# Two chained attention blocks on one core: one weight quarter loaded earlier, six weight pieces later, and the second output projection started eight units later

## The chip, the cores and the metric

The kernel runs on one core of a Trainium2 chip. The metric is the device time of one execution in microseconds (us); lower is better. A kernel with rounds is compared with the kernel before on the same chip in the same rounds. One execution of each kernel was taken by the hardware profiler.

Engines in the profile: PE is the matrix engine (PEld its weight loads), ACT the scalar engine, DVE the vector engine, POOL the general engine, SP the engine that issues all loads and stores. SPq is SP's queue.

## The reference, cut to what matters

Two independent problems A and B of the same shape; their outputs are put side by side.

```python
B, Sq, D = 16, 144, 448          # batch, queries, model width
H, Sk, Dh = 16, 512, 256         # heads, cached keys, head width
q = (x @ wq).reshape(B, Sq, H, Dh).transpose(0, 2, 1, 3)
scores = jnp.einsum("bhqd,bhkd->bhqk", q, k_cache) * (Dh ** -0.5)
p = softmax(scores)
o = jnp.einsum("bhqk,bhkd->bhqd", p, v_cache)
y = o.transpose(0, 2, 1, 3).reshape(B, Sq, H * Dh) @ wo      # all bf16
```

## The kernel before

The kernel works through 512 *units*. A unit is one batch and head: 0 to 255 are problem A, 256 to 511 problem B. For each unit the matrix engine does Q (x times wq), S (K times q), PV (V times the exponentials) and, a little later and two matmuls at a time, a piece of the output projection OP (with wo). ACT makes the exponentials and the reciprocals of the sums, DVE moves results out of PSUM, POOL adds up the exponentials. Each engine plays a fixed list of instructions; the order is decided when the program is built.

Every load goes through SP's one queue. There are four kinds at the place where the problems meet, which this text calls the *join*:

- a K wave: the keys of 16 units, transposed on the way; wave n is for units 16n to 16n+15, and there is room for two waves
- a V group: the values of two units; V group n is for units 2n and 2n+1, with nine slots
- a wq quarter (four heads) and a wo piece (two heads, eight pieces), each kept once, so that B's overwrites A's as soon as A is done with it

```python
RS = 3                                        # chunks of 128 output rows in the ring
OP_DELAY, OP_START, OP_START_B = 2, 28, 20
# ...
# the order of the loads at the join: k = K wave, v = V group, q = wq quarter of B, o = wo piece of B
MID = ("k16 v127 v128 q0 v129 v130 q1 v131 q2 q3 v132 k17 v133 v134 v135 v136 v137 o0 o1 v138 o2 v139 o3 v140 o4 v141 "
       "o5 v142 o6 o7 k18")
# ... t_load_k: one transposing DMA of a whole wave
src = ks[pr].rearrange("b h (p c) d -> (b h p) (c d)", c=4)[r0 * 128:(r0 + KW) * 128, :]
q.dma_start_transpose(kt_sb[:, :, sl * KW * 128:(sl + 1) * KW * 128], src)
# ... t_load_wq, t_load_wo: into the one buffer of both problems
q.dma_start(wq_sb[:, 0:3, cols], w[0:384, cols].rearrange("(c p) n -> p c n", p=128))
q.dma_start(wo_sb[:, c0:c0 + WOG, :], w[c0 * 128:(c0 + WOG) * 128, :].rearrange("(c p) n -> p c n", p=128))
# ... where MID goes into the plan of all loads
for lo, rank, _n, fn, args in loads:
    if (fn, args) == mid[0]:
        dma_plan.extend(mid)
# ... the step from which a pair of projection matmuls may be placed
ready = max(i + OP_DELAY, OP_START if pr == 0 else pr * NU + OP_START_B)
```

## Time and profile before

| what | before |
|---|---|
| median time of the first 3 runs, us | 1057.1 |
| span of the profiled run, us | 1055.3 |
| PE busy, us | 1031.0 |
| PE waits on loads at the join, us | 3.6 (wq quarter 0) and 2.9 (K wave 18) |
| short PE waits on DVE's q, us | 1.5 |

The head of the page: span, and busy time of each engine with its share of the span.

```profile
span 1055.3 us, 32320 instructions
PE 1031.0 (98%) x12376; PEld 875.0 (83%) x12376; DVE 740.9 (70%) x2039; ACT 793.9 (75%) x2365; POOL 636.6 (60%) x1030
```

The matrix engine bounds the kernel, so only its idle time and its slow clock can be won. The waits of PE; columns are who waited, for whom, total us, times, longest us:

```profile
PE qp_ps L1052 <- DMA wq_sb<-in_B_wq_dram: 3.6, 1, 3.6
PE s_ps L1086 <- DMA kt_sb<-in_B_k_cache_dram: 2.9, 1, 2.9
PE s_ps L1086 <- DVE qt_sb L1066: 1.5, 5, 0.4
```

Line 1052 is Q, 1086 is S, 1142 is PV, 1259 is OP. The first line is the first Q of B, which waits for its weights. The second is the first S of wave 18. Busy time by stretches (stretch, its length, busy us and instructions of each engine, granted clock of PE, mean busy share of the load engines, GB/s) shows where it is. (The share of the load engines is the time of all packets over that of 16 engines; it can exceed 1.)

```profile
500.00:560.00 60.00, 56.39 (x690) 48.08 (x687) 43.64 (x105) 43.33 (x130) 35.42 (x58) 0.97 1.18 286
560.00:600.00 40.00, 38.99 (x466) 33.03 (x464) 30.28 (x73) 30.44 (x91) 24.90 (x41) 1.00 1.16 318
600.00:650.00 50.00, 47.08 (x524) 38.52 (x522) 32.36 (x96) 34.78 (x104) 27.93 (x46) 0.97 1.17 294
650.00:1000.00 350.00, 349.77 (x4077) 293.78 (x4076) 250.07 (x681) 272.99 (x818) 222.78 (x358) 1.00 1.19 281
```

From 650 to 1000 us PE is busy for 349.77 of 350 us; at the join it is not, and its clock is lower. (Most of the other idle time, 9.7 us in the first 40 us and 6.5 us in the last 36, is the start and the end of the kernel, which the change leaves alone.) The timeline of PE around the first wait (start, us, what, times; in brackets the idle time before it) shows why the clock counts too:

```profile
530.18 1.39 PE L1052 MATMUL qp_ps<-xt_sb,wq_sb 128*128 128x288 bf16 x8 [3.58 <-DMA wq_sb<-in_B_wq_dram]
531.37 1.17 PE L1086 MATMUL s_ps<-qt_sb,kt_sb 128*128 128x144 bf16 x8
...
534.75 0.66 PE L1086 MATMUL s_ps<-qt_sb,kt_sb 128*128 128x144 bf16 x8
```

After the wait the eight matmuls of S take 1.17 us, and 0.66 us a little later. The clock record of the trace has the clock at one half for 3.4 us after each of the two waits; by estimate that costs 1.7 us each. This is the clock gate of the Trainium skill, "TensorE: Matmul & The Clock Gate", Part 1, which names an idle window of about 3.4 us; here waits of 3.6 and 2.9 us did it. Lastly, the SP queue around waves 18 and 19 (start and length of the issue; the length includes waiting, and the issue of a transpose lasts nearly as long as the transfer):

```profile
577.60 2.44 SPq L933 DMA_DIRECT2D wo_sb<-in_B_wo_dram  x2
580.09 21.07 SPq L960 DMA_TRANSPOSE kt_sb<-in_B_k_cache_dram  x1
601.20 0.58 SPq L1288 DMA_DIRECT2D out_dram<-ost_sb  x1
601.83 5.65 SPq L973 DMA_DIRECT2D v_sb<-in_B_v_cache_dram  x8
607.52 7.42 SPq L948 DMA_TRANSPOSE xt_sb<-in_B_x_dram  x1
614.98 1.44 SPq L949 DMA_TRANSPOSE xt_sb<-in_B_x_dram  x1
616.46 16.97 SPq L960 DMA_TRANSPOSE kt_sb<-in_B_k_cache_dram  x1
```

All eight wo pieces are ahead of wave 18 (the issue at 580); between it and wave 19 (616) there are only V groups, a store and x. Taking the landing of every load from the trace, each load adds a nearly constant time to the landing of the one before it while the queue is full: about 17.4 us for a K wave, 1.36 for a V group, 3.3 for a wq quarter, 1.2 for a wo piece.

### The profile page before, as it was taken

To read this page: it belongs to the slowest core of one execution; us is meant where nothing else is said; L and a number is where in the kernel's file an instruction comes from. 1 tells how busy PE (TensorE), PEld (TensorE's weight loads), DVE (VectorE), ACT (ScalarE), POOL (GpSimd) and SP (SyncE) were. 2 spreads that over 40 slices of the span, in tenths; PEclk is the share of its full clock that TensorE was granted. 3 is DMA by queue.
4 is the path that set the end of the run, shared out by engine and by line. 5 is a ranking of instruction groups with operands and counts; after the bars stand their busy time and mean duration, and the time that the engine had idled before them with its cause. 6 is when DMAs were issued, how large, how long until landed. Compare 5 with 4: busy or idle time off the path is not lost.

```text
span 1055.3 us, 32320 instructions
## 1 busy us (share of the span) xinstructions
PE 1031.0 (98%) x12376; PEld 875.0 (83%) x12376; DVE 740.9 (70%) x2039; ACT 793.9 (75%) x2365; POOL 636.6 (60%) x1030
## 2 busy tenths in 40 slices
PE   6999999999999999999999899999999999999997
PEld 6999888888888888888878788888888888888885
DVE  4776666776766777777868667677776667777775
ACT  4887667777777777878857667777877777788785
POOL 3554556656666566666746556566666666666673
PEclk9999999999999999999999999999999999999999
DMA  9999999999999999999999999999999999999960
GB/s 316 372 343 291 294 291 248 283 299 271 264 305 260 248 286 262 304 289 280 283 281 343 279 283 287 303 284 292 251 279 280 278 286 298 296 254 274 292 201 14
DMA packets 589060, 294.15 MB, mean 279 GB/s; under 512 B 500832, under 2 KB 513632, under 8 KB 588896
## 3 DMA queue, kind: packets, MB, share of 16 engines
q1 hardware_dynamic: 588896, 291.99, 110.9%
q8 instruction: 99, 1.62, 0.6%
q14 instruction: 65, 0.53, 0.2%
HBM read 161.48 MB, written 4.13 MB: 157 GB/s over the span
## 4 chain that ended last, share of the span: by engine, by line
PE 91%; DMA 5%; ACT 1%; DVE 1%; SPq 1%; issue 0%; POOL 0%; ACTq 0%; DVEq 0%
PE s_ps L1086 23%; PE ot_ps L1142 23%; PE qp_ps L1052 22%; PE op_ps L1259 19%; DMA kt_sb<-in_B_k_cache_dram 2%; DMA v_sb<-in_A_k_cache_dram 2%; PE ot_ps L1158 2%; PE s_ps L1000 1%; PE qp_ps L1000 1%; DMA wq_sb<-in_B_wq_dram 1%; PE qp_ps L1259 1%; ACT rinv_sb L1179 0%; ACT pt_sb L1096 0%; DVE ring L1194 0%; DVE qt_sb L1066 0%
## 5 line engine op out<-in xcount | busy, mean ns | idle before, releaser
L1106 POOL TENSOR_TENSOR pp_sb<-pt_sb 128x288 f32<-128x288 bf16 x512 | 384.9, 752 | 322.5 <-ACT pt_sb L1096 308.1
L1096 ACT ACTIVATE pt_sb<-s_ps 128x288 bf16<-128x288 f32 x1024 | 364.6, 408 | 184.4 <-PE s_ps L1086 177.6
L1194 DVE TENSOR_TENSOR ring<-ot_ps,rinv_sb 128x288 bf16<-128x288 f32 (+2 forms) x640 | 241.9, 394 | 150.3 <-ACT rinv_sb L1179 145.8
L1086 PE MATMUL s_ps<-qt_sb,kt_sb 128*128 128x144 bf16 x4096 | 341.3, 226 | 4.7 <-DMA kt_sb<-in_B_k_cache_dram 2.9
L1142 PE MATMUL ot_ps<-pt_sb,v_sb 128*128 128x144 bf16 x4096 | 340.3, 226 | 0.0
L1086 PEld LDWEIGHTS s_ps<-qt_sb,kt_sb 128*128 128x128 bf16 x4096 | 287.7, 98 | 56.9 <-DVE qt_sb L1066 5.6
L1179 ACT ACTIVATE rinv_sb<-ln_sb 64x144 f32<-64x144 f32 x928 | 298.3, 321 | 24.3
L1052 PE MATMUL qp_ps<-xt_sb,wq_sb 128*128 128x288 bf16 (+1 forms) x2368 | 302.3, 271 | 6.6 <-DMA wq_sb<-in_B_wq_dram 3.6
L1259 PE MATMUL op_ps<-wo_sb,ring 128*128 128x448 bf16 x1120 | 285.2, 353 | 0.0
L1052 PEld LDWEIGHTS qp_ps<-xt_sb,wq_sb 128*128 128x128 bf16 x2368 | 212.3, 98 | 81.9 <-issue 7.5
L1142 PEld LDWEIGHTS ot_ps<-pt_sb,v_sb 128*128 128x128 bf16 x4096 | 274.5, 98 | 0.5
L1111 POOL TENSOR_TENSOR p_sb<-pp_sb 128x144 f32<-128x144 f32 x464 | 227.5, 490 | 74.6 <-DVE ps_sb L1120 10.4
L1209 DVE TENSOR_REDUCE run_sb<-ot_ps 128x1 bf16<-128x144 f32 x560 | 146.5, 304 | 79.4 <-ACT ln_sb L1166 44.3
L1120 DVE TENSOR_TENSOR ps_sb<-p_sb 64x144 bf16<-64x144 f32 x464 | 158.7, 342 | 44.4 <-POOL p_sb L1111 30.3
L1066 DVE CAST qt_sb<-qp_ps 128x576 bf16<-128x576 f32 x216 | 162.1, 751 | 21.3 <-PE qp_ps L1052 17.7
L1259 PEld LDWEIGHTS op_ps<-wo_sb,ring 128*128 128x128 bf16 x1120 | 94.0, 98 | 21.2
L1166 ACT ACTIVATE ln_sb<-ot_ps 128x144 f32<-128x144 f32 x232 | 67.9, 293 | 32.6 <-PE ot_ps L1158 25.3
L1158 PE MATMUL ot_ps<-ps_sb,ones 128*128 128x144 bf16 x280 | 63.4, 226 | 0.0
L1065 DVE CAST qt_sb<-qp_ps 128x288 bf16<-128x288 f32 x80 | 35.9, 448 | 4.8 <-PE qp_ps L1052 4.3
L1008 ACT ACTIVATE kt_sb<-qp_ps 128x512 bf16<-128x512 bf16 x48 | 28.9, 603 | 7.3 <-PE qp_ps L1000 7.3
L1111 POOL TENSOR_TENSOR ps_sb<-pp_sb 128x144 bf16<-128x144 f32 x48 | 23.5, 490 | 6.9 <-PE ot_ps L1158 0.3
L1158 PEld LDWEIGHTS ot_ps<-ps_sb,ones 128*128 128x128 bf16 x280 | 27.5, 98 | 0.0
(29 smaller groups left out, 153.4 us busy)
## 6 DMA issues: line engine op xcount, KB each, us to landing
v_sb<-in_A_v_cache_dram SPq DMA_DIRECT2D x128, 512.0 KB, 7.1
v_sb<-in_B_v_cache_dram SPq DMA_DIRECT2D x128, 512.0 KB, 7.5
v_sb<-in_A_k_cache_dram SPq DMA_DIRECT2D x24, 512.0 KB, 9.6
out_dram<-ost_sb SPq DMA_DIRECT2D x36, 112.0 KB, 6.2
wo_sb<-in_A_wo_dram SPq DMA_DIRECT2D x8, 448.0 KB, 8.7
wo_sb<-in_B_wo_dram SPq DMA_DIRECT2D x8, 448.0 KB, 9.0
wq_sb<-in_A_wq_dram SPq DMA_DIRECT2D x4, 768.0 KB, 10.1
wq_sb<-in_B_wq_dram SPq DMA_DIRECT2D x4, 768.0 KB, 10.6
```

What stands on the lines that cost most here:

```text
L1052: ins = t.matmul(acc, lhsT=wq_sb[:, kc, c0:c0 + 128], rhs=xt_sb[:, kc, xo:xe + 1:max(xe - xo, 1), :], start=(kc == 0), stop=(kc == 3))
L1066: return v.tensor_copy(qt_sb[:, a:b + 1:b - a, :, :], qp_ps[:, :, 0:2 * SQ].rearrange("p e (u q) -> p u e q", u=2))
L1086: ins = t.matmul(s_ps[bank][:, (c % 2) * SQ:(c % 2 + 1) * SQ], lhsT=kt_sb[:, 2 * c + dc, ko:ko + 128], rhs=qt_sb[:, qsl, dc, :], start=(dc ...
L1096: return a.activation(pt_sb[:, psl, 2 * k:2 * k + 2, :].rearrange("p b q -> p (b q)"), s_ps[bank][:, 0:2 * SQ], AF.Exp, scale=DH ** -0.5)
L1106: return g.tensor_tensor(pp_sb[:, :, :], pt_sb[:, psl, 0:2, :], pt_sb[:, psl, 2:4, :], op=ALU.add)
L1111: return g.tensor_tensor(dst, pp_sb[:, 0, :], pp_sb[:, 1, :], op=ALU.add)
L1120: return v.tensor_tensor(ps_sb[p0:p0 + 64, sl, :], p2_sb[0:64, :], p2_sb[64:128, :], op=ALU.add)
L1142: ins = t.matmul(ot_ps[ob][:, dc * SQ:(dc + 1) * SQ], lhsT=v_sb[:, vsl, j, c * DH + dc * 128:c * DH + (dc + 1) * 128], rhs=pt_sb[:, sl, c, ...
L1179: return a.activation(rinv_sb[p0:p0 + 64, sl, :], ln_sb[h0:h0 + 64, :], AF.Exp, scale=-1.0)
L1194: ins = v.tensor_tensor(ring[:, 2 * h:2 * h + 2, r0:r0 + q1 - q0], ot_ps[ob][:, 0:2 * SQ].rearrange("p (c q) -> p c q", c=2)[:, :, q0:q1], ...
L1209: return v.tensor_reduce(run_sb[:, k, j:j + 1], ot_ps[ob][:, 2 * SQ:3 * SQ], axis=AX.X, op=op)
L1259: ins = t.matmul(acc[0:m, 0:D], lhsT=ring[:, c, col0:col0 + m], rhs=wo_sb[:, c, :], start=(c == first), stop=(c == last))
```

## The change

The intent: B's first Q should not wait for its weights, so wq quarter 0 goes ahead of wave 16. Wave 18 should not wait behind all of wo, so six of the eight wo pieces go behind it, one between every two V groups. The projection of B needs those pieces, so it begins at unit 28 of B instead of 20. No arithmetic and no byte is added or removed.

```diff
-    OP_DELAY, OP_START, OP_START_B = 2, 28, 20
+    OP_DELAY, OP_START, OP_START_B = 2, 28, 28
@@
-    MID = ("k16 v127 v128 q0 v129 v130 q1 v131 q2 q3 v132 k17 v133 v134 v135 v136 v137 o0 o1 v138 o2 v139 o3 v140 o4 v141 "
-           "o5 v142 o6 o7 k18")
+    MID = ("q0 k16 v127 v128 v129 q1 v130 v131 q2 v132 q3 k17 v133 v134 v135 v136 v137 v138 v139 o0 v140 o1 v141 "
+           "k18 v142 o2 v143 o3 v144 o4 v145 o5 v146 o6 v147 o7")
@@
-            if (fn, args) == mid[0]:
+            if (fn, args) == (t_load_k, (16,)):
                 dma_plan.extend(mid)
```

## The prediction

> **What bounds it now.** The matrix engine: the page shows PE busy 1031.0 us of a 1055.3 us span (98%). In the busy-time-by-stretch view it is over 99% busy from 40 to 520 us and from 610 to 1020 us. The idle time the change can reach lies at the join of the two problems, 520 to 610 us. The wait view gives two DMA waits there: the first second-problem Q for its wq quarter (3.6 us, at 526) and the first S of K wave 18 (2.9 us, at 602). After each, matmul groups run at about half rate for some 3 us (S took 1.17 us instead of 0.66; granted clock 0.95 to 0.96 in these stretches), about 1.7 us lost each. The Trainium skill ("TensorE: Matmul & The Clock Gate", Part 1) says an idle window of about 3.4 us halves the clock; this trace agrees. So wq costs about 5.5 us and wave 18 about 5 us. While no output projection is ready (569 to 583), a pair of units takes 3.54 us against 3.04 us of matmul (timeline): 0.5 us lost per pair, 2 us in all.
>
> **What limits there is the DMA queue.** All loads go through one queue, and by the issue and landing times they land in order, each adding a nearly constant time while the queue is full: K wave 17.4 us, V pair 1.36, wq quarter 3.3, wo piece 1.2. From 500 to 645 us the queue hardly empties; one wave (K plus eight V) is 28 us of some 32 us of matmul.
>
> **What changes.** No arithmetic, no bytes. wq quarter 0 goes ahead of K wave 16, and must wait for the first problem's last Q of that quarter (about 505 us, where wave 16 was issued at 500): a bubble of about 1 us. Six of eight wo pieces go behind wave 18. Projection starts 8 units later.
>
> **Cost and gain.**
> 1. The wq wait at 526 vanishes: -5.5 us.
> 2. But V group 133, behind wave 17, landed at 563.7 and was needed at 565.0: 1.3 us of slack. What is ahead of it in the queue (wave 16, four wq quarters, V 127 to 132, wave 17) is the same set in another order. It lands about 1 us later, and the matrix engine arrives 5.5 us earlier: a wait of 4 to 6 us plus a slow clock, partly perhaps at wq quarter 1. Gain 1 is given back: +6 to +7.
> 3. Wave 18 has 7 to 8 us less ahead of it: its wait and slow clock vanish: -4.5.
> 4. Four more pairs without projection: +2. The deferred projection (28 matmuls, 5 us) is done later, where the matrix engine is the limit.
> 5. Wave 19 has the same total ahead of it and had 2.4 us of slack (landed 636.0, needed 638.3); the matrix engine comes 3 to 5 us earlier: +1 to +4.
>
> Sum about +1.5: **1058.5 us, range 1053 to 1064**. Chances: faster by over 2% 0.01, within 2% 0.98, slower 0.01.
>
> **What would show it.** No Q wait on wq quarter 0; a new wait of 3 to 6 us of PV on a second-problem V load near 560 us, with half clock after it; no wave-18 wait; a small wave-19 wait near 635 us; projection absent for about 28 us instead of 14; matrix busy time unchanged.
>
> **What would make it wrong.** If loads overlap more than the landings suggest, V 133 is on time and the gain is 5 to 9 us. If the V wait is split into short ones, no slow clock follows and time falls about 2 us. If the bubble is larger, waits grow at wave 16 too: 4 us slower.

(Its landing times count from a start 0.3 us later than the timeline's; differences are not touched by that. This trace agrees with the idle window that it cites only for the wait of 3.6 us; the wait of 2.9 us, which halved the clock too, is shorter.)

## The result, and the profile after

| what | before | after |
|---|---|---|
| median, us (6 runs each, same rounds) | 1055.98 | 1064.68 |
| lowest to highest, us | 1054.45 to 1058.32 | 1064.51 to 1067.4 |
| ratio after to before, 95% interval | | 1.0078, 1.0062 to 1.0095 |
| span of the profiled run, us | 1055.3 | 1062.9 |

A ratio here is the mean time of one kernel's fast runs over the mean of the other's of the same rounds, so it is not quite the ratio of the medians. The change made the kernel slower by 0.8%, 8.2 us by the ratio. The prediction's 1058.5 us, with its range to 1064, was too low. The page's head, the waits and the stretches, in the same order:

```profile
span 1062.9 us, 32320 instructions
PE 1031.5 (97%) x12376; PEld 875.5 (82%) x12376; DVE 742.4 (70%) x2039; ACT 793.7 (75%) x2365; POOL 634.5 (60%) x1030
```

```profile
PE s_ps L1086 <- DMA kt_sb<-in_B_k_cache_dram: 5.5, 1, 5.5
PE ot_ps L1142 <- DMA v_sb<-in_B_v_cache_dram: 4.0, 2, 2.7
PE qp_ps L1052 <- DMA wq_sb<-in_B_wq_dram: 3.0, 1, 3.0
...
PE s_ps L1086 <- DVE qt_sb L1066: 2.4, 8, 0.4
...
PE qp_ps L1052 <- DVE qt_sb L1066: 0.3, 1, 0.3
```

```profile
500.00:560.00 60.00, 56.95 (x698) 48.58 (x696) 44.46 (x107) 43.35 (x130) 35.21 (x57) 0.97 1.15 267
560.00:600.00 40.00, 34.80 (x432) 29.94 (x429) 31.41 (x72) 30.23 (x92) 24.79 (x40) 1.00 1.18 290
600.00:650.00 50.00, 43.34 (x476) 35.62 (x477) 29.00 (x91) 31.52 (x95) 25.50 (x41) 0.97 1.13 314
650.00:1000.00 350.00, 349.77 (x4053) 292.73 (x4051) 247.65 (x673) 269.66 (x809) 218.71 (x353) 1.00 1.18 281
```

PE's busy time is the same (1031.5 against 1031.0 us), so all the loss is idle time, and it lies at the join. The wait on wq quarter 0 is gone, and so is the wait on wave 18. In their place stand a wait on wq quarter 1 (the single wq line, at 537 us), two on V groups (133 for 2.7 us, 142 for 1.35 us), and a wait of 5.5 us on wave 19, with half clock after it, which the timeline of PE shows:

```profile
640.82 1.12 PE L1086 MATMUL s_ps<-qt_sb,kt_sb 128*128 128x144 bf16 x8 [5.53 <-DMA kt_sb<-in_B_k_cache_dram]
641.73 1.16 PE L1142 MATMUL ot_ps<-pt_sb,v_sb 128*128 128x144 bf16 x8
```

The loss adds up from these lines, with an estimated 1.7 us for each half-clock stretch of 3.4 us. Both kernels have two such stretches, so the slow clock cancels in the difference:

| at the join, us | before | after |
|---|---|---|
| wq quarter 0, with slow clock | 3.6 + 1.7 | 0 |
| wq quarter 1, with slow clock | 0 | 3.0 + 1.7 |
| V groups 133 and 142 | 0 | 4.0 |
| wave 18, with slow clock | 2.9 + 1.7 | 0 |
| wave 19, with slow clock | 0 | 5.5 + 1.7 |
| short waits on DVE's q (whole run) | 1.5 | 2.7 |
| sum | 11.4 | 18.6 |

The difference of the sums, 7.2 us, is nearly the difference of the spans, 7.6 us.

The SP queue shows where wave 19 stands now (wo is line 933, the two transposes of line 960 are waves 18 and 19), and the chain of waits, in its last line here, how long wave 19 took from issue to landing:

```profile
574.06 22.84 SPq L960 DMA_TRANSPOSE kt_sb<-in_B_k_cache_dram  x1
596.94 0.58 SPq L973 DMA_DIRECT2D v_sb<-in_B_v_cache_dram  x1
597.56 0.47 SPq L933 DMA_DIRECT2D wo_sb<-in_B_wo_dram  x1
...
608.16 0.56 SPq L933 DMA_DIRECT2D wo_sb<-in_B_wo_dram  x1
608.77 3.22 SPq L973 DMA_DIRECT2D v_sb<-in_B_v_cache_dram  x3
612.03 7.38 SPq L948 DMA_TRANSPOSE xt_sb<-in_B_x_dram  x1
...
620.92 17.70 SPq L960 DMA_TRANSPOSE kt_sb<-in_B_k_cache_dram  x1
```

```profile
620.92 19.77 DMA kt_sb<-in_B_k_cache_dram
```

Wave 19 can be checked by hand. After the change it lands 41.8 us after wave 18 (31.5 before), mostly because six wo pieces (7.2 us at the constant times above) and V 142 (1.4 us) now stand between the two; the last 1.6 us no count of bytes explains. PE takes 32.5 us from the first S of wave 18 to where it wants wave 19, and wave 18 had landed 3.9 us before its own first S. 41.8 - 32.5 - 3.9 = 5.4 us, the wait that the profile shows.

There is a second way to see the same loss. At the first S of wave 19 the two kernels are only 2.2 us apart in time (640.82 and 638.63 us), but by the traces the changed kernel has then done 624 projection matmuls and the kernel before 644. The 20 missing ones, at 0.19 us each (six take 1.14 us in the chain of waits), are done later, where PE has no idle time: 3.8 us more. The half clock that still runs for 3.0 us after this point adds about 1.5 us: 7.5 us in all. So the matrix engine was relieved of work just where it had to wait for loads anyway.

### The profile page after: what moved, and what is told of

Same layout as the page of the kernel before. It is cut to its first block, busy times and chain, and to the rows that moved or that the text cites. A ratio compares the mean times of both kernels' runs of the same rounds, so it can differ in the third digit from the quotient of the medians.

```text
span 1062.9 us, 32320 instructions
## 1 busy us (share of the span) xinstructions
PE 1031.5 (97%) x12376; PEld 875.5 (82%) x12376; DVE 742.4 (70%) x2039; ACT 793.7 (75%) x2365; POOL 634.5 (60%) x1030
## 4 chain that ended last, share of the span: by engine, by line
PE 90%; DMA 5%; ACT 2%; DVE 2%; SPq 1%; issue 0%; POOL 0%; ACTq 0%; DVEq 0%
PE s_ps L1086 23%; PE ot_ps L1142 23%; PE qp_ps L1052 22%; PE op_ps L1259 19%; DMA kt_sb<-in_B_k_cache_dram 2%; PE ot_ps L1158 2%; DMA v_sb<-in_A_k_cache_dram 1%; PE s_ps L1000 1%; DMA wq_sb<-in_B_wq_dram 1%; ACT rinv_sb L1179 1%; DMA v_sb<-in_B_v_cache_dram 1%; PE qp_ps L1000 1%; PE qp_ps L1259 1%; DVE ring L1194 1%; DVE qt_sb L1066 1%; ACT pt_sb L1096 0%
```

## The experiments

Theory: at the join the one load queue sets the pace ("queue theory"). Moving a load ahead only moves the wait to another load, and moving projection work out of the join gives the queue less time to catch up. Rivals: the later projection alone does the harm, or the load order alone; the waits come from late slots and not from the length of the queue.

### One part at a time

Only the first half of the new order, with the old second half and the old start:

```diff
-    MID = "k16 v127 v128 q0 v129 v130 q1 v131 q2 q3 v132 k17 v133 ..."        # rest as before
+    MID = "q0 k16 v127 v128 v129 q1 v130 v131 q2 v132 q3 k17 v133 ..."        # rest as before
```

> Only the first part of the change: wq quarter 0 ahead of K wave 16 (and the V/wq order that goes with it); wo pieces and the start of the second output projection as before. Queue theory (the join is limited by the one load queue, so moving a load moves the wait): same waits as the changed kernel up to 570 us (Q on wq quarter 1 about 3.0 us with half clock after it, PV on V 133 about 2.7 us, no wait on quarter 0), then wave 18 is later by 3 to 4 us and is waited for 4 to 6 us; total 2 to 4 us over before. Rival (the delayed projection alone is to blame, the wq move is a gain): 3 to 6 us below before.

Measured: 1058.27 us, before 1056.1 us; ratio 1.0018, interval 0.9996 to 1.0039, so a loss is not shown by itself; a gain of 3 to 6 us, as the rival has it, is excluded. Its waits:

```profile
PE ot_ps L1142 <- DMA v_sb<-in_B_v_cache_dram: 4.2, 1, 4.2
...
PE qp_ps L1052 <- DMA wq_sb<-in_B_wq_dram: 2.1, 1, 2.1
PE s_ps L1086 <- DMA kt_sb<-in_B_k_cache_dram: 1.7, 1, 1.7
```

The gain that the wq move was made for does not come: the wait goes to wq quarter 1 and V 133. The total is as the queue theory had it, at its low end; the wave-18 wait of 1.7 us is below the 4 to 6 us that I expected; the 6.3 us waited for before it may have given it time.

Only the later start, on the old load order:

```diff
-    OP_DELAY, OP_START, OP_START_B = 2, 28, 20
+    OP_DELAY, OP_START, OP_START_B = 2, 28, 28
```

> Only OP_START_B 20 -> 28, load order as before. Queue theory: wq quarter 0 wait 3.6 us as before; the matrix engine reaches wave 18 about 2.6 us earlier (28 deferred matmuls of 0.19 us, less 2 us more idling between pairs), so wave 18 is waited for 5 to 6 us instead of 2.9; the deferred matmuls come later on a full matrix engine: total 3 to 5 us over before. Rival (the load order alone is to blame): within 1 us of before, or at most the 2 us of idling.

Measured: 1059.49 us, ratio 1.0030, interval 1.0007 to 1.0054. The wq wait is 3.2 us, the wave-18 wait 3.7 us (5 to 6 expected). The later start costs about 3 us by itself. Its wave-18 wait:

```profile
PE s_ps L1086 <- DMA kt_sb<-in_B_k_cache_dram: 3.7, 1, 3.7
```

The later start and the spread wo, but wq in its old places:

```diff
-    MID = "k16 v127 v128 q0 v129 ... o6 o7 k18"
+    MID = ("k16 v127 v128 q0 v129 v130 q1 v131 q2 q3 v132 k17 v133 v134 v135 v136 v137 v138 v139 o0 v140 o1 v141 "
+           "k18 v142 o2 v143 o3 v144 o4 v145 o5 v146 o6 v147 o7")                # and OP_START_B = 28
```

> wo spread behind wave 18 and projection 8 units later, but the wq quarters in their old places. Queue theory: wq quarter 0 wait 3.6 us as before, no wait on wave 18, a wait of about 1 us on V 142 and of 4 to 6 us on wave 19; total 4 to 7 us over before, 1 to 3 us under the changed kernel. If the wq move does the harm alone: within 1 us of before.

Measured: 1062.92 us, ratio 1.0060, interval 1.0037 to 1.0083. wq quarter 0 is waited for 4.9 us, wave 19 for 5.3 us (the line below), wave 18 and V 142 not at all.

```profile
PE s_ps L1086 <- DMA kt_sb<-in_B_k_cache_dram: 5.3, 1, 5.3
```

By the ratios this is 3.2 us above the run with the later start alone (their intervals overlap), so the spread of wo seems to cost more than the wait on wave 18 that it takes away. From V 126 to wave 19 the queue took nearly the same time in the two profiles, 129.8 and 130.2 us: the order did not change when wave 19 could land, but which wave was waited for.

The new load order, with the start back at 20:

```diff
-    OP_DELAY, OP_START, OP_START_B = 2, 28, 28      # the changed kernel
+    OP_DELAY, OP_START, OP_START_B = 2, 28, 20
```

> The changed load order with the projection start put back to 20. The wo pieces 2 to 7 land only from 602 us on, while the projection needs the third piece some three units after its start (about 586 us): the matrix engine, in order, waits for wo for 8 to 16 us at once, and everything behind it with it. Queue theory: total 6 to 12 us over before, no wait on wave 19. Rival (the later start does the harm): below the changed kernel by 3 us or more.

Measured: 1068.25 us, ratio 1.0109, interval 1.0088 to 1.0131, slower than the changed kernel. One wait explains it:

```profile
PE op_ps L1259 <- DMA wo_sb<-in_B_wo_dram: 11.5, 1, 11.5
```

So the later start was not a mistake next to the new order of wo: with wo behind wave 18, an earlier start makes PE wait for wo. The two belong together, and together they lose.

### The loads themselves

Four kernels cut B's weight loads to 64 of their columns (of wq also only the first and the last of its four row blocks) and leave all else, so that the queue has less to carry. B's result is then wrong; A's weights stand in. The comparison found the three with wo cut wrong; with wq alone cut it passed, so it does not notice the wrong wq.

```diff
+            nn = D if pr == 0 else 64                                             # wo
-                return q.dma_start(wo_sb[:, c0:c0 + WOG, :], ...)
+                return q.dma_start(wo_sb[:, c0:c0 + WOG, 0:nn], ...)
@@
+                if pr:                                                            # wq
+                    c1 = slice(hg * 4 * DH, hg * 4 * DH + 64)
+                    q.dma_start(wq_sb[:, 0:1, c1], ...)
+                    return q.dma_start(wq_sb[64:128, 3, c1], ...)
```

Both cut, in the kernel before and in the changed kernel:

> The kernel before with the second problem's wq and wo loads cut to 64 columns (wrong result for the second problem on purpose; the first problem's weights stay in place). Queue theory: about 20 us of queue time go, so no DMA wait over 0.3 us at the join, no half clock there; 9 to 11 us below before (3.6 + 2.9 of waits, 3.4 of slow clock). Rival (the waits at the join have another cause than queue length, such as late slots): waits on K waves or V stay.

> The changed kernel with the same cut (wrong on purpose). Queue theory: no DMA wait at the join either; the only thing left of the change is four more pairs without projection, 0.5 us of idling each: 1.5 to 3 us over the kernel before with the same cut. Rival (the later projection is harmful by itself, through the deferred matmuls, with or without a full queue): 4 to 6 us over it.

Measured: 1047.74 us (ratio 0.9923, 0.9903 to 0.9943) and 1047.39 us (ratio 0.9918, 0.9898 to 0.9939), both against before at 1055.44 us. The waits of PE on loads at the join: one of 0.7 us on wq left in the first, none in the second. So the queue's length makes the waits, and it costs the kernel before some 8 us. The two are now equal: my expectation of 1.5 to 3 us for the later start was wrong. The short waits on DVE do grow (the second kernel's line; its line numbers are six higher for the added code),

```profile
PE s_ps L1092 <- DVE qt_sb L1072: 2.4, 8, 0.4
```

by 1.0 us on this line against the first of the two, but the first still has its 0.7 us wait on wq. With a free queue the change costs nothing that these runs can show.

Only wq cut, in the changed kernel:

> The changed kernel with only the wq loads of the second problem cut (wrong on purpose); wo whole. Queue theory: some 11 us less ahead of V 133, wave 18 and wave 19, so the waits on V 133, V 142 and wave 19 all vanish: within 1 us of the changed kernel with both cut. If wave 19 is late because of the wo pieces behind wave 18 instead: a wave-19 wait of 2 us or more stays.

Measured: 1047.73 us, ratio 0.9920, interval 0.9899 to 0.9940. The waits on V are gone; a wave-19 wait of 2.0 us stays in the profiled execution, but that one took 1050.01 us, and the other three took 1047.01 to 1048.16 us, so it may not be in every execution. It left open whether wo between the waves is enough with wq whole. So the other half was run, wo cut and wq whole:

> The changed kernel with only the second problem's wo loads cut to 64 columns (wrong on purpose); wq whole. If wave 19 is late because six wo pieces (7.3 us) stand between waves 18 and 19: 33 to 36 us from wave 18 to wave 19 instead of 41.8, the waits on wq quarter 1 and V 133 stay (5 to 7 us with half clock), the wave-19 wait of 5.5 us is gone or under 1 us; 1054 to 1058 us. If the wait is inherited from the wq quarters ahead of wave 16: 2 us or more of it stays.

Measured: 1056.72 us, the same as before in its rounds (1056.61 us; ratio 1.0000, interval 0.9978 to 1.0022). The waits of PE on loads at the join are these two and no other:

```profile
PE qp_ps L1053 <- DMA wq_sb<-in_B_wq_dram: 3.2, 1, 3.2
...
PE ot_ps L1143 <- DMA v_sb<-in_B_v_cache_dram: 2.7, 1, 2.7
```

Wave 19 lands 36.5 us after wave 18 instead of 41.8, a little above the 33 to 36 that I wrote down, and is not waited for. The waits that the wq quarters make are untouched. Without the bytes of wo ahead of wave 19 its wait is gone, and it is worth nearly all of what the change lost: the changed kernel is then as fast as the kernel before. The second way of counting gives the same: PE reaches wave 19 3.6 us earlier than in the kernel before (635.06 us), with 20 projection matmuls, 3.8 us, left over; the spans are 1055.4 and 1055.3 us.

Two limits. This run cuts all eight pieces, and two of them are ahead of wave 18 too; and the run before it, with wq cut ahead of both waves, removed most of the same wait. So these two show that the bytes ahead of wave 19 make its wait, not that they must stand between the two waves. That the order decides which wave is waited for is shown by the two runs with the later start alone and with the spread (3.7 us on wave 18, then 5.3 us on wave 19).

### Is the head of the queue blocked, or is it chance?

From the landing of V 126 to that of wave 19 the same loads took 129.1 us before and 134.1 us after, 5 us that no count of bytes explains. In the changed kernel SP stands from 499 to 504.6 us before wq quarter 0, until A's last Q of that quarter has run; behind it, wave 16 can't be issued, though its slot is free. One kernel puts the quarter right behind the wave:

```diff
-    MID = ("q0 k16 v127 v128 v129 q1 ..."
+    MID = ("k16 q0 v127 v128 v129 q1 ..."                                         # rest as after
```

> The changed kernel with wq quarter 0 right behind K wave 16 instead of right ahead of it, nothing else. In the changed kernel the queue head waits from 499 to 504 us for the last Q of the first problem, and the queue takes 134.1 us from V 126 to wave 19, against 129.1 before, for the same loads. If that blocked head is the cause of the 5 us: 129 to 131 us here, a wait of about 1 us on wq quarter 0, wave-19 wait 2 to 4 us, total 2 to 4 us under the changed kernel. If the interleaving of small and large loads is the cause: 133 us or more and the same total within 1 us.

Measured: 1062.67 us, ratio 1.0073, interval 1.0052 to 1.0094, 131.5 us in the queue. The wq wait is 1.0 us, the V 133 wait 3.0 us, the wave-19 wait 5.5 us. By medians it is 2 us under the changed kernel, by the ratios half a us, with other rounds for the two; so the blocked head is at most a small part. Neither forecast was met: the time in the queue fell by 2.6 us, and the wave-19 wait stayed, because PE came 2.8 us earlier as well.

Both kernels unchanged, for a second profile:

> The kernel before, unchanged, for a second profile: how much the queue's time from V 126 to K wave 19 (129.1 us) varies from one execution to the next. If it stays within 1 us of 129.1, the 134.1 us of the changed kernel belong to its load order; if it varies by 3 us or more, they are chance.

> The changed kernel, unchanged, for a second profile: within 1 us of 134.1 us from V 126 to K wave 19 if its load order makes the queue slower; nearer 130 us if the first profile was chance. The wave-19 wait should be 4 to 6 us in either case, as its total time is steady.

Measured, one run each (state unknown): 1060.74 us with 132.2 us in the queue, and 1064.1 us with 132.7 us. The kernel before, whose runs here lie between 1053.1 and 1061.0 us, waited longer in this execution:

```profile
PE s_ps L1086 <- DMA kt_sb<-in_B_k_cache_dram: 4.7, 1, 4.7
PE qp_ps L1052 <- DMA wq_sb<-in_B_wq_dram: 4.6, 1, 4.6
```

The changed kernel had the wave-19 wait again, at 5.5 us:

```profile
PE s_ps L1086 <- DMA kt_sb<-in_B_k_cache_dram: 5.5, 1, 5.5
PE ot_ps L1142 <- DMA v_sb<-in_B_v_cache_dram: 4.1, 1, 4.1
```

So the queue's time for the same loads in the same order moves by 3 us from one execution to the next. How much of the 5 us belongs to the new order and how much to chance stays open, though by the rule written down before (3 us or more) it would be called chance. In this second pair of profiles wave 19 landed at nearly the same time in both kernels, 639.8 us before and 640.2 us after, and the changed kernel was still 3.4 us longer in span: PE reached wave 19 2.6 us earlier, but with the 20 projection matmuls (3.8 us) left over and about 2.4 us of slow clock to come (estimated from the 4.7 us of half clock left there).

### The other way round

If work taken out of the join costs, work brought into it should pay. The kernel before with its projection six units earlier:

```diff
-    OP_DELAY, OP_START, OP_START_B = 2, 28, 20
+    OP_DELAY, OP_START, OP_START_B = 2, 28, 14
```

> The kernel before, its load order untouched, with the second output projection starting 6 units earlier (20 -> 14), the opposite of the change. Queue theory: the matmuls that come earlier run in time that the join spends waiting for loads anyway: wq wait about 3.6 us as before, the idling between pairs (1.0 us in the profile of before) nearly gone, the wave-18 wait 1 to 2 us shorter, later some 14 to 20 matmuls (3 to 4 us) fewer left to do: 1.5 to 4 us below before. Rival (the start of the projection does not matter, the load order does): within 1 us of before.

Measured: 1055.94 us against 1056.59 us, ratio 0.9986, interval 0.9963 to 1.0010: no gain shown. In its profile the wq wait was 5.5 us, more than in the first profile of before. Wave 18 was not waited for at all (a wait 1 to 2 us shorter was expected), but wave 19 was, for 2.9 us, and a later K wave for 1.2 us; wave 19 took 35.7 us from the landing of wave 18, in the same load order that took 31.5 us before. The short waits on DVE fell to 0.5 us as expected.

The same with V 127 ahead of wave 16, V 133 ahead of wave 17, the wo pieces a little earlier, and the projection of A two units later from unit 96 on:

```diff
-    OP_DELAY, OP_START, OP_START_B = 2, 28, 20
+    OP_DELAY, OP_START, OP_START_B = 2, 28, 14
@@
+    MID = ("v127 k16 v128 q0 v129 v130 q1 v131 q2 q3 v132 v133 k17 v134 v135 v136 v137 v138 o0 o1 o2 o3 "
+           "v139 v140 o4 v141 o5 o6 v142 o7 k18")
@@
-    ready = max(i + OP_DELAY, ...)
+    ready = max(i + (4 if pr == 0 and u >= 96 else OP_DELAY), ...)
```

> As e11_before_op14, with V 133 ahead of wave 17, the wo pieces a little earlier, and the first problem's projection two units later, so that it reaches up to the second's. Queue theory: the order in the queue only moves the wait, so within 1 us of e11_before_op14. A gain of 2 us or more over it would say that order alone can pay.

Measured: 1053.01 us against 1056.59 us, ratio 0.9967, interval 0.9942 to 0.9992. It is the only correct version here that beats both kernels, by 0.3%. Its waits in the profiled execution (which at 1050.19 us was its fastest):

```profile
PE qp_ps L1052 <- DMA wq_sb<-in_B_wq_dram: 3.6, 1, 3.6
...
PE s_ps L1086 <- DMA kt_sb<-in_B_k_cache_dram: 1.1, 1, 1.1
...
PE s_ps L1086 <- DVE qt_sb L1066: 0.2, 1, 0.2
```

Its interval and that of the simpler kernel overlap, so which of its edits pays beside the earlier start is not told apart. It is 2.0 us under that kernel by the ratios, just what I had said would show that order alone can pay; that is not shown.

## Why the prediction was right or wrong

- *PE bounds the kernel, the join holds its idle time*: right. Busy time moved by 0.5 us; nearly the whole loss lies between 500 and 650 us (7.4 us more idle time there).
- *Step 1, the wq wait vanishes*: right for quarter 0.
- *Step 2, the gain is given back at V 133, partly at quarter 1, +6 to +7*: right in place, a little low in size. 3.0 us on quarter 1, 1.7 of slow clock after it, 2.7 on V 133: 7.4 us. The run with only this part of the change shows the same places. V 133 landed 2.9 us later than before (566.9 against 564.0 us) where the step had about 1; here that hardly showed, in step 5 it did.
- *Step 3, the wave-18 wait vanishes, -4.5*: right, 2.9 + 1.7 us. That V 142, now behind wave 18, would be waited for (1.35 us) was not foreseen; the second profile of the changed kernel lacks it.
- *Step 4, +2 for the pairs without projection*: too large. The short waits grew by 1.2 us, and with the queue relieved the two kernels took the same time. At wave 19 it was 20 matmuls that were left for later, not 28.
- *Step 5, wave 19: "+1 to +4"*: this is the term that failed. It measured 5.5 us of wait and 1.7 us of slow clock, 7.2 us where the sum had about 2.5. That PE would come 3 to 5 us earlier was right: it wanted wave 19 3.3 us earlier than before. But the step let wave 19 land only some 1 us later, as the total ahead of it was the same, each load at a constant time. It landed 4.4 us later (640.7 against 636.3 us): 3.3 + 4.4 - 2.4 of slack is the wait. Of the 4.4 us, 2.9 us were there at V 133 already, ahead of every moved wo piece. The constant times came from one profile, and a second one of the same kernel is 3 us longer over these loads and has wave 19 land at 639.8 us. The prediction should have given that landing a spread as wide as the slack it was compared with, and the half clock that a long wait brings. Cutting the wo loads took the wave-19 wait and 8 us away: that the bytes ahead of wave 19 make its wait is shown; the split of the 4.4 us between the new order and chance is not.
- *Matrix busy time unchanged, no wave-18 wait, a V wait near 560 us, projection absent for longer*: as foreseen, but the half clock fell behind quarter 1 and not behind V 133 in the first profile, and behind V 133 in the second.

## What to carry to other kernels

Where one in-order queue of loads sets the pace, as here, moving a load ahead mostly moves the wait; cutting bytes there took it away. (Loads brought forward into a stretch with room might too; no run here tried that alone.) Look at every deadline behind the place where a load is put, not only at the one it is taken away from: six pieces moved from before one deadline to before the next took one wait away and made a longer one. And leave the bounding engine its deferrable work in the stretch where it must wait, since work pushed out of it is paid in full later.

## What the Trainium skill lacked or had wrong

- "TensorE: Matmul & The Clock Gate", Part 1, gives an idle window of about 3.4 us before the clock halves, measured by a free-running window. Here shorter waits did it: 2.9 us (wave 18, before) and 3.0 us (wq quarter 1, after), while a wait of 2.7 us (V 133, after) did not in one execution. In the run with only wo cut a wait of 2.7 us on V 133 did, and a wait of 2.86 us on wave 19 with the projection at 14 did not, so the length of the wait alone does not decide here. The half clock lasted 3.4 us, or 6.8 us in some profiles (around the V 133 wait of 4.2 us in the first experiment), or 10.2 us around the wo wait of 11.5 us.
- "DMA: Bandwidth & Descriptors", Latency and other measured facts, gives a transposing load 261 GB/s with a non-contiguous middle dimension and about 350 to 400 GB/s when contiguous. Here a K wave of 4.19 MB took about 17.4 us in a full queue, 241 GB/s by that division and below both figures, next to plain V groups of 0.52 MB in 1.36 us, 385 GB/s.
- The same page, Queues, rings and completion order, warns that completion is not in order of issue. In this trace the loads at the join landed in order of issue. No page that I read says how much the time of one unchanged sequence of loads varies: here 129.1 and 132.2 us in two executions of one kernel, and 15.7 to 19.4 us for one K wave in another.
